# Transposing q and k on VectorE in 32x32 squares instead of on TensorE, in a fused attention and SwiGLU kernel

## The chip, the core and the metric

The kernel runs on one NeuronCore of a Trainium2 chip. The metric is the device time of one execution in microseconds (us), here the median of three runs.

The engines have short names in the profile: PE is TensorE (PEld its weight loads), DVE is VectorE, ACT is ScalarE, POOL is GpSimd, SP is SyncE, which computes nothing and issues most of the DMA transfers. The transfers themselves are carried out by 16 DMA engines.

## The reference

Attention with a threshold, 8 batches of 8 heads, 576 positions of 64, all float32; then a SwiGLU layer over the 4,608 rows of 512 that the heads make together.

```python
scores = scale * np.matmul(q, k.transpose(0, 1, 3, 2))          # 576 x 576 per head
thresh = np.max(scores, axis=-1, keepdims=True) - tau           # tau = 0.02
scores = np.where(scores >= thresh, scores, -1000000000.0)
attn = np.exp(scores - np.max(scores, axis=-1, keepdims=True))
attn = attn / (np.sum(attn, axis=-1, keepdims=True) + 1e-09)
x = np.matmul(attn, v)                                          # -> (B * S, H * D)
xn = x / rms(x) * rms_g
out = (silu(xn @ w_gate) * (xn @ w_val)) @ w_out                # 512 -> 1536 -> 512
```

## The kernel before, in words

**Tiling.** Heads are worked on in pairs, p = 0 to 3 (one head on partitions 0 to 63, the other on 64 to 127). Of the 576 rows of a batch 512 are "main" and 64 are the "tail". The main rows make four chunks of 128 queries; the tails of two batches together make one more chunk. So there are 36 chunks, and 36 x 4 pairs = 144 steps, in the order of `chunks` and `steps` (L249 to L263). A step is one chunk of queries of one head pair against all 576 keys.

**A step.** TensorE makes the scores of both heads (L601). From step 32 to step 143 this is done in bursts of 1,024 columns per head that fill `s_ps`, two times two PSUM banks; the next burst can start when VectorE has read the last one. VectorE copies the scores out and takes their minimum after a scale of -1/8 (L634). POOL adds tau (L675). ScalarE, and POOL for one head in every third step, make the weights (L686, L693, L705, L719, L724) in `wsb`, of which there are three. SP issues a DMA transpose of the weights into `wt`, of which there are five (L753; the first 16 steps use TensorE). TensorE multiplies them by v (L771, L776), VectorE normalises (L793, L794).

**The layer behind it.** When a chunk's four steps are done, ScalarE, POOL and a DMA transpose (L823) make its normalised, transposed rows. Groups of four chunks (two at first) then go through the layer: TensorE L877 and L882, ScalarE L891, VectorE L894 and L899, TensorE L948 (L923 in the last, streamed group), an eviction at L961 or L963, and a store at L968, or L972 for a tail chunk.

**How q and k get there.** TensorE needs both with the 64 elements of a head on the partitions. For batches 1 to 7 `emit_qk` (L307) loads k and q of a pair by one transfer each, 128 partitions by 8 pieces of 64 float32 (L316), into one of three buffers `qkn`. TensorE transposes them by 16 matmuls with an identity, 64x64 each (L326), into two banks of a ring of PSUM banks. VectorE copies one bank into `qkt` (L339), ScalarE the other (L337). The k tails of a batch are loaded by one transfer and transposed by `emit_k_tail` (L456, L461, L473), the q tails of two batches by `emit_q_tail` (L481, L485, L495). Batch 0 has its own code, `emit_first` (L347).

**How v gets there.** `emit_v` (L501) loads v of a pair by one transfer of 128 partitions by 2 pieces of 1 KB (L521), and the tails by two transfers (L533); POOL casts to float16 (L509).

**What sets the order.** Every operation is an `Op` with an engine, an assumed cost (`COST`, `DMA_NS`), a due step (`prio`) and the operations it depends on. `order_ops` (L55) plays a list schedule with these costs and writes down one fixed order per engine; `RANK` (L26) shifts the due steps of kinds of operations, for those due from step 8 on. Each engine then runs its order strictly, waiting at an instruction until its operands are there. SP's order holds the loads, the transposes of L753 and L823, and the stores. A load of a batch's inputs is held back to a step (`gated`, and L1057): `emit_batch_inputs` (L544) sets 3.3 steps from pair to pair, and loads three steps ahead of that. The buffers of `qkn` are free for a new load when the transposition three blocks back is done. TensorE's score matmuls run either over 128 queries at once or over two times 64 (`o.quad`, L1065); the first is taken where another operation with half-height tiles, such as a transposition, follows.

Of the kernel before, what the change touches and what calls it, by code (L numbers as in the profile page):

```python
# [19 lines left out]
    pool_tiny=302.0, pool_mean=944.0, pool_dma=880.0, cast_v=620.0, cast_vt=475.0, cast_w=665.0,  # L20
    sp=420.0, sp_v=600.0, sp_w=600.0, sp_tr=1300.0, sp_qk=680.0, sp_tl=630.0,
)
DMA_NS = dict(qk=1250.0, tl=700.0, v=880.0, vt=350.0, wt=1700.0, xt=800.0, out=800.0, w=820.0, wo=2500.0)
SWITCH = 125.0

RANK = dict(  # L26
    ACT={"emit_ffn/ev": -70, "emit_ffn/store": 10, "emit_ffn/tanh": -150, "emit_k_tail/ev": 60, "emit_q_tail/ev": -60, "emit_qk/ev": -20,
        "emit_softmax/ex": 70, "emit_softmax/ex2": 63, "emit_softmax/prelu": 140, "emit_x/sq": -20},
    DVE={"emit_av/half": -110, "emit_burst/ttr": 14, "emit_ffn/ev": -100, "emit_ffn/silu": 20, "emit_k_tail/ev": -70, "emit_qk/ev": 16,
        "emit_softmax/ev": 50},  # L30
    PE={"emit_burst/fn": -29, "emit_ffn/gmm": 8, "emit_ffn/omm": 10, "emit_ffn/vmm": -34, "emit_k_tail/tr": -100, "emit_q_tail/tr": 100, "emit_qk/tr":
        -10, "emit_softmax/tr": -130},
    POOL={"emit_softmax/mask": 60, "emit_softmax/nthr": 60, "emit_softmax/take": -10, "emit_x/mean": 110, "emit_x/norm": -60, "round_/<lambda>": 90,
        "main/<lambda>": 150, "main/cast": 10},
)
# [19 lines left out]
def order_ops(ops, ring_sizes):  # L55
# [4 lines left out]
    for o in ops:  # L60
        if o.prio >= 8.0 and o.eng != "SP":
            path = o.fn.__qualname__.split(".")
            o.prio += RANK[o.eng].get((path[-3] if path[-3].startswith(("emit", "load", "setup", "transposed", "round")) else "main") + "/" + path[-1], 0.0)

# [15 lines left out]
    out = []  # L80
    ready_at = {i: 0.0 for i in range(len(ops))}
    while len(out) < len(ops):
# [35 lines left out]
        if o.ring is not None:  # L118
            o.slot = []
            for _ in range(o.nring):  # L120
                got = min(f for f in ring_free[o.ring] if f[1] in (o.pick or SLOTS))
                ring_free[o.ring].remove(got)
                o.slot.append(got[1])
        eng_free[e] = t + cost
        if o.dma:
# [21 lines left out]
def kernel(  # L147
# [29 lines left out]
    def ps(name, n):  # L177
# [9 lines left out]
    wo = sb("wo", [128, NFC, DM], FP16)  # L187
    qkn = [sb(f"qkn{i}", [128, 2, 4, 2, D]) for i in range(NQK)]
    qtl = [sb(f"qtl{i}", [128, H, D]) for i in range(2)]
    ktl = [sb(f"ktl{i}", [128, H, D]) for i in range(2)]  # L190

    qkt = [sb(f"qkt{i}", [128, NP, 2 * S]) for i in range(2)]
    qkT = [[t[:, p].rearrange("p (j s) -> p j s", j=2)[:, :, 0:MAIN].rearrange("p j (c n) -> p j c n", n=128)
            for p in range(NP)] for t in qkt]
    kT = [[[t[:, p, S:2 * S], t[:, p, MAIN:MAIN + S]] for p in range(NP)] for t in qkt]
    kTt = [[t[:, :, S + MAIN:2 * S], t[:, :, MAIN:S]] for t in qkt]
    qTv = [sb(f"qTv{i}", [128, NP, 128]) for i in range(2)]
    va = [sb(f"va{i}", [128, NP, 10, D + 1], FP16) for i in range(2)]
# [107 lines left out]

    def emit_qk(b, p, prio):  # L307
        dst = qkT[b % 2][p]
        n = len(tr_of[0])
# [11 lines left out]
        def tr(o):  # L321
            for j in (1, 0):
                for c in range(4):
                    for r, rs in enumerate(HALF):
                        at = 256 * j + 64 * c
                        nc.tensor.transpose(ring[o.slot[r]][:, at:at + 64],  # L326
                                            nat[rs, j, c].rearrange("s h d -> s (h d)"), id32[rs, rs])
# [16 lines left out]
        for c in range(4):  # L344
            qk_ready[b, p, c] = done

    def emit_first():  # L347
# [63 lines left out]
        def emit_k(p, load, prio):  # L411
            nat = qkn[p % NQK]
            t, k_ready[p] = transposed(load, [pair(nat[:, 1, c]) for c in range(4)],
                                       [(0, 2, qkT[0][p][:, 1, 0:2]), (2, 2, qkT[0][p][:, 1, 2:4])], prio,
                                       [("ACT" if p in (1, 2) else "DVE", 0, 2), ("ACT", 2, 4)])
            tr_of[1].append(t)

        emit_k(0, lo, -20)
        _, q0_ready[0] = transposed(lq, [pair(q0[:, 0:2])], [(0, 1, qkT[0][0][:, 0, 0:1])], -21, [("DVE", 0, 1)])
        tk, kt_first = transposed(lt, [pair(ktl[0][0:64, 0:2])], [(0, 1, kTt[0][h][HALF[h], 0:1]) for h in range(2)], -19, [("ACT", 0, 1)])  # L420
# [3 lines left out]
        tq, got = transposed(lq2, [pair(q0[:, 2 * p:2 * p + 2]) for p in range(1, NP)],  # L424
                             [(p - 1, 1, qkT[0][p][:, 0, 0:1]) for p in range(1, NP)], -9, [("DVE", 0, 1), ("ACT", 1, 3)])
        q0_ready[1:] = [got[:1], got[1:], got[1:]]
# [8 lines left out]
        for p in range(NP):  # L435
            nat = qkn[p % NQK]
            t, got = transposed(load_q(p, (-23, -22, -19, -18)[p]), [pair(nat[:, 0, c]) for c in range(1, 4)],
                                [(0, 3, qkT[0][p][:, 0, 1:4])], p + 2.0, [(EVAC[p % 2], 0, 3)])
            tr_of[0].append(t)
            for c in range(4):  # L440
                qk_ready[0, p, c] = k_ready[p] + (got if c else q0_ready[p])
# [59 lines left out]
    def emit_v(b, prio):  # L501
# [13 lines left out]
        for p in range(NP):  # L515
# [4 lines left out]
            def load(o, p=p, nat=nat):  # L520
                nc.sync.dma_start(out=nat, in_=main[:, 2 * p:2 * p + 2])  # L521

            lo = gated(add("SP", COST["sp_v"], pr, v_cast[n - len(vst):n - len(vst) + 1] if n >= len(vst) else [], load,
                           dma=DMA_NS['v'], bulk=True), pr)
# [5 lines left out]
            if p == 0:  # L530
                def load_tail(o):
                    for e in range(2):
                        nc.sync.dma_start(out=vtl[64 * e:64 * e + 64], in_=hv[e, MAIN:S])  # L533

                lo = gated(add("SP", 2 * COST["sp_tl"], pr + 0.3, vt_cast[-2:], load_tail, dma=DMA_NS['vt'], bulk=True), pr + 0.3)
                for e in range(2):
                    es = slice(64 * e, 64 * e + 64)
                    ca = add("POOL", COST["cast_vt"], (pr + 1.3 if b else -0.5), [lo] + [x for p in range(NP) for x in free(p)],
                             round_(t[es, :, 8 + e, 0:D], vtl[es]))
                    vt_cast.append(ca)  # L540
                    for p_ in range(NP):
                        v_ready.setdefault((b, p_), []).append(ca)

    def emit_batch_inputs(b):  # L544
        base = first_step[b - 1] if b else -10
        if b == 1:
            base += B1_BASE
        emit_tail_load(b, base + (4 if b else 1))
        if b == 0:
            q0_use.extend(emit_first())  # L550
        else:
            for p in range(NP):
                pr = base + 3.3 * p + 3
                emit_qk(b, p, pr)
                if p == 0:
                    emit_k_tail(b, pr + 2)
        emit_v(b, base + 5 if b else -1)
        if b % 2:
            emit_q_tail(b // 2, v_step[b // 2] - 1.5)
# [9 lines left out]
    def parts_of(s):  # L569
        ci, p = steps[s]  # L570
        kind, b, c = chunks[ci]
        if kind == "m":
            deps = qk_ready[b, p, c] + kt_ready[b, p]
            whole = [(slice(0, 128), b % 2, lambda hs: qkT[b % 2][p][hs, 0, c])]
            quads = [(rs, b % 2, lambda hs, rs=rs: qkT[b % 2][p][hs, 0, c, rs]) for rs in HALF]
            return deps, whole, quads
        deps = list(qv_ready[b])
        quads = []
        for e in range(2):
            deps += qk_ready[2 * b + e, p, 0] + kt_ready[2 * b + e, p]  # L580
            quads.append((HALF[e], e, lambda hs, e=e: qTv[b % 2][hs, p, HALF[e]]))
        return deps, None, quads
# [4 lines left out]
    def emit_burst(segs, prio, runs):  # L587
# [5 lines left out]
        for run in runs:  # L593
            def fn(o, run=run):
                for s, lo, hi, at in run:
                    _, whole, quads = info[s]
                    p = steps[s][1]
                    for rows, i, lhs in quads if no_whole or o.quad else whole:
                        for h in range(2):
                            hs = HALF[h]  # L600
                            nc.tensor.matmul(s_ps[h][rows, at:at + hi - lo], lhs(hs), kT[i][p][h][hs, lo:hi],  # L601
                                             start=True, stop=True)
# [251 lines left out]
    def emit_ffn(slot, parts, ready_step, pace, streamed):  # L854
# [81 lines left out]
        for j, (ci, _) in enumerate(parts):  # L936
# [28 lines left out]
            def store(o, oi=oi, kind=kind, b=b, c=c, late=late):  # L965
                if kind == "m":
                    dst = out[b * S:b * S + MAIN].rearrange("(si sc) d -> si sc d", sc=4)[:, c]
                    (nc.scalar if late else nc.sync).dma_start(out=dst, in_=osb[oi])  # L968
                else:
                    for e in range(2):  # L970
                        r0 = (2 * b + e) * S + MAIN
                        nc.sync.dma_start(out=out[r0:r0 + TAIL], in_=osb[oi][64 * e:64 * e + 64])  # L972

# [141 lines left out]
NSTAGE = 3  # L1115
NQK = 3
W_FROM = 2.0
W_STEP = 0.4
# [42 lines left out]
```

## Time and profile before

| what | value |
|---|---|
| three runs | 547.73, 549.47, 551.49 us; median 549.47 |
| the profiled execution: its own time | 549.99 us |
| its span (first to last instruction) | 548.0 us |
| granted TensorE clock | 0.998 of full speed |
| POOL busy | 256.4 us (47%) |
| DMA packets | 270,022, of which 252,544 under 512 B |
| read from and written to HBM | 37.75 and 9.44 MB |
| block loads (L316), issue to landing | 3.4 / 4.3 / 7.8 us (shortest, median, longest) |
| weight transposes (L753), issue to landing | 3.2 / 3.6 / 7.8 us |
| who waited for the weight transposes | POOL 1.1 us, ACT 0.7 us |
| longest waits by kind | POOL L675 for VectorE 169.9 us; VectorE L634 for TensorE L601 39.1 us; ScalarE L891 for TensorE L877 31.2 us |

How to read the profile. "Busy" is the time in which an engine's instructions ran, whatever they waited for inside. Matmuls are pipelined, so that a busy TensorE isn't TensorE at its peak. A group's line gives source line, engine, operation, output and inputs with shape, count, then busy us and mean ns of one, then idle time of the engine just ahead of such instructions. A DMA queue's line gives packets, megabytes, and the time that its packets took as a share of all 16 engines over the span or window; q1 holds what SP issues, q10 what ScalarE issues. The sum of packets in flight can pass 1.0. The chain of work is followed back from the last instruction, at each step to what released it.

### The profile page before, as it was taken

To read this page: it belongs to the slowest core of one execution; us is meant where nothing else is said; L and a number is where in the kernel's file an instruction comes from. 1 tells how busy PE (TensorE), PEld (TensorE's weight loads), DVE (VectorE), ACT (ScalarE), POOL (GpSimd) and SP (SyncE) were. 2 spreads that over 40 slices of the span, in tenths; PEclk is the share of its full clock that TensorE was granted. 3 is DMA by queue.
4 is the path that set the end of the run, shared out by engine and by line. 5 is a ranking of instruction groups with operands and counts; after the bars stand their busy time and mean duration, and the time that the engine had idled before them with its cause. 6 is when DMAs were issued, how large, how long until landed. Compare 5 with 4: busy or idle time off the path is not lost.

```text
span 548.0 us, 14515 instructions
## 1 busy us (share of the span) xinstructions
PE 536.8 (98%) x5420; PEld 295.8 (54%) x5420; DVE 452.7 (83%) x1300; ACT 441.8 (81%) x684; POOL 256.4 (47%) x418
## 2 busy tenths in 40 slices
PE   8998999999999999999999999999999999999996
PEld 4765676664555455645555556555655454545442
DVE  4997998888997799789987998699979987995562
ACT  5998989988998789788979898879988988793221
POOL 2367833763645434654554454644644544451000
PEclk9999999999999999999999999999999999999999
DMA  8999999979997797998898789999998567564201
GB/s 195 262 256 277 185 177 224 144 164 200 181 161 160 153 155 160 202 194 148 173 196 165 111 160 206 220 171 166 175 202 151 104 97 150 92 127 82 79 0 77
DMA packets 270022, 89.03 MB, mean 162 GB/s; under 512 B 252544, under 2 KB 262272, under 8 KB 269952
## 3 DMA queue, kind: packets, MB, share of 16 engines
q1 hardware_dynamic: 267024, 85.76, 81.9%
q0 software_dynamic: 1600, 1.57, 2.0%
q8 instruction: 42, 0.69, 0.5%
q10 hardware_dynamic: 1328, 0.79, 0.5%
q14 instruction: 28, 0.23, 0.2%
HBM read 37.75 MB, written 9.44 MB: 86 GB/s over the span
## 4 chain that ended last, share of the span: by engine, by line
PE 80%; DVE 5%; DMA 4%; POOL 4%; issue 3%; ACT 3%; SPq 0%; POOLq 0%; DVEq 0%; ACTq 0%
PE s_ps L601 25%; PE ring L948 14%; PE ring L877 14%; PE ring L882 14%; PE ring L776 5%; DVE ssb L634 3%; PE ring L771 2%; PE ring L326 2%; PE s_ps L923 2%; DMA stg<-in_moe_w_gate_dram 1%; POOL wsb L719 1%; ACT ssb L686 1%; DMA vst<-in_v_dram 1%; PE s_ps L882 1%; POOL wsb L724 1%
## 5 line engine op out<-in xcount | busy, mean ns | idle before, releaser
L686 ACT ACTIVATE ssb<-ssb,nth 128x576 f32<-128x576 f32 x246 | 180.8, 766 | 28.1 <-POOL nth L675 27.5
L634 DVE CUSTOM_DVE_ANT_0 ssb<-s_ps,zrow 128x576 f32<-128x576 f32 (+8 forms) x288 | 172.0, 635 | 10.6 <-PE s_ps L601 8.8
L601 PE MATMUL s_ps<-qkt 64*64 64x288 f32 (+17 forms) x1636 | 154.7, 415 | 1.8 <-DVE mx L634 1.1
L693 ACT ACTIVATE wsb<-ssb 128x1152 f16<-128x1152 f32 x102 | 118.2, 1159 | 1.6
L675 POOL TENSOR_SCALAR nth<-mx 128x2 f32<-128x2 f32 x144 | 31.6, 219 | 178.0 <-DVE mx L634 169.9
L877 PE MATMUL ring<-xnT,wg 128*128 128x512 f16 (+1 forms) x472 | 111.1, 358 | 0.1
L601 PEld LDWEIGHTS s_ps<-qkt 64*64 64x64 f32 (+1 forms) x1636 | 77.8, 146 | 60.2 <-issue 26.0
L882 PE MATMUL ring<-xnT,wv 128*128 128x512 f16 (+1 forms) x456 | 107.0, 357 | 0.5 <-DVE qkt L339 0.3
L891 ACT ACTIVATE th<-ring 128x512 f32<-128x512 f32 (+1 forms) x118 | 63.9, 541 | 31.6 <-PE ring L877 31.2
L894 DVE SCALAR_TENSOR_TENSOR sl<-th,ring 128x512 f32<-128x512 f32 (+1 forms) x118 | 73.9, 628 | 13.8 <-ACT th L891 13.5
L634 DVE CUSTOM_DVE_ANT_0 ssb<-s_ps,zrow,mxp 128x128 f32<-128x128 f32 (+7 forms) x112 | 53.4, 514 | 31.0 <-PE s_ps L601 30.3
L719 POOL TENSOR_SCALAR wsb<-ssb,nth 128x576 f16<-128x576 f32 x42 | 72.5, 1726 | 4.8 <-DMA wt<-wsb 1.1
L882 PEld LDWEIGHTS <-wv 128*128 128x128 f16 x480 | 45.6, 98 | 49.8 <-issue 6.4
L877 PEld LDWEIGHTS <-wg 128*128 128x128 f16 x480 | 42.8, 97 | 40.7 <-issue 4.4
L724 POOL TENSOR_TENSOR wsb<-wsb,esb 128x576 f16<-128x576 f16 x42 | 53.7, 1278 | 6.1 <-ACT esb L705 3.1
L776 PE MATMUL ring<-va,wt 128*128 128x65 f16 (+1 forms) x1264 | 50.3, 193 | 0.0
L776 PEld LDWEIGHTS <-wt 128*128 128x128 f16 (+1 forms) x1280 | 46.2, 100 | 3.0 <-issue 0.4
L948 PE MATMUL ring<-wo,hf 128*128 128x512 f16 x204 | 47.5, 379 | 0.0
L899 DVE TENSOR_TENSOR hf<-ring,sl 128x512 f16<-128x512 f32 (+1 forms) x59 | 37.3, 635 | 4.5 <-PE s_ps L601 0.5
L948 PE MATMUL ring<-wo,stg 128*128 128x512 f16 x168 | 39.1, 379 | 0.0
L705 ACT ACTIVATE esb<-ssb,nth 128x576 f16<-128x576 f32 x42 | 32.3, 770 | 7.9 <-POOL nth L675 7.9
L899 DVE TENSOR_TENSOR stg<-ring,sl 128x512 f16<-128x512 f32 (+1 forms) x55 | 34.6, 631 | 4.0
(76 smaller groups left out, 552.8 us busy)
## 6 DMA issues: line engine op xcount, KB each, us to landing
vst<-in_v_dram SPq DMA_DIRECT2D x32, 256.0 KB, 3.4
qkn<-in_k_dram SPq DMA_DIRECT2D x31, 256.0 KB, 4.3
out_dram<-osb SPq DMA_DIRECT2D x29, 256.0 KB, 2.9
qkn<-in_q_dram SPq DMA_DIRECT2D x28, 256.0 KB, 4.5
stg<-in_moe_w_gate_dram SPq DMA_DIRECT2D x6, 512.0 KB, 6.3
stg<-in_moe_w_val_dram SPq DMA_DIRECT2D x6, 512.0 KB, 5.9
wt<-wsb SPq DMA_TRANSPOSE x128, 3.6
wo<-in_moe_w_out_dram POOLq DMA_DIRECT2D x4, 384.0 KB, 6.3
```

The lines of the kernel that those rows point to most:

```text
L601: nc.tensor.matmul(s_ps[h][rows, at:at + hi - lo], lhs(hs), kT[i][p][h][hs, lo:hi], start=True, stop=True)
L634: nc.vector.tensor_tensor_reduce(out=ssb_of(s)[:, h, lo:hi], in0=s_ps[h][:, at:at + hi - lo], in1=zrow[:, lo:hi], scale=-1.0 / 8.0, scalar ...
L686: nc.scalar.activation(out=sb_[:, h], in_=sb_[:, h], func=PRELU, scale=-1.0, bias=nth[m][:, h:h + 1], **PRELU_KW)
L693: nc.scalar.activation(out=wsb[s % NW], in_=sb_, func=AF.Exp)
L719: nc.gpsimd.tensor_scalar(out=wsb[s % NW][:, h], in0=sb_[:, h], scalar1=nth[m][:, h:h + 1], scalar2=None, op0=ALU.is_le)
L776: nc.tensor.matmul(ring[o.slot[0]][rs, at:at + D + 1], w[:, 5 * h + j, rs], va[vi][:, p, 2 * j + h], start=False, stop=(h == 1 and j == 3))
L877: nc.tensor.matmul(ring[o.slot[0]][:, 0:n], wg[d][:, fs], xnT[slot][:, d, 0:n], start=(d == 0), stop=(d == 3))
L882: nc.tensor.matmul(ring[o.slot[0]][:, 0:n], wv[d][:, fs], xnT[slot][:, d, 0:n], start=(d == 0), stop=(d == 3))
L891: nc.scalar.activation(out=th[i][:, 0:n], in_=ring[g.slot[0]][:, 0:n], func=AF.Tanh, scale=0.5)
L894: nc.vector.scalar_tensor_tensor(out=sl[i][:, 0:n], in0=th[i][:, 0:n], scalar=1.0, in1=ring[g.slot[0]][:, 0:n], op0=ALU.add, op1=ALU.mult)
L899: nc.vector.tensor_tensor(out=hf[hi][:, 0:n], in0=ring[vv.slot[0]][:, 0:n], in1=sl[i][:, 0:n], op=ALU.mult)
L948: nc.tensor.matmul(ring[(first or o).slot[0]], hf[hs[fc][0]][:, 128 * j:128 * (j + 1)], wo[:, fc], start=(fc == 0), stop=(fc == NFC - 1))
```

## The change

From batch 2 on (`BLOCKED = 2`) `emit_qk` hands over to `emit_blocks`. Each head's q and k are loaded by a transfer of its own, 64 partitions by 18 pieces of 32 float32: partition 32 e + s takes half e (32 elements) of the 18 rows 18 s to 18 s + 17. The main part and the tail come together. Three VectorE transposes of 32x32 squares then write `qkt`: one for k, one for q (512 columns each), one for the tails of both (192 columns). The buffers `qkn` become `qkx`, 1,216 float32 wide; `qkt` gets 64 more columns, and k now stands ahead of q in it.

The queries and keys of a chunk are therefore other rows than before, and v and the output follow: v of a pair is loaded by two transfers, each of 4 times 32 pieces of 1 KB in DRAM, its tails by four transfers of 32 partitions, and a chunk is stored as 4 times 32 rows (a tail chunk as 2 times 32 for each of its batches). The separate loads and TensorE transposes of the tails are gone for batches 2 to 7, and TensorE reads the queries of tail chunks from `qkt`.

Two more edits: where an operation takes several PSUM banks from a given list (the last group's four accumulators), it takes them in rising order ("banks sorted"); and `COST`, `DMA_NS` and the whole of `RANK` have other values, so that the written-down order differs on every engine. The diff, cut to its core:

```diff
+    qkx = [sb(f"qkx{i}", [128, 2 * S + TAIL]) for i in range(NQK)]
+    qkt = [sb(f"qkt{i}", [128, NP, 2 * S + TAIL]) for i in range(2)]
+    RUN = S // 32
+    LEAD = (0, RUN - MAIN // 32)
+    TAIL_AT = (MAIN // 32, 0)
+    def rows_of(x):
+        return x.rearrange("(s r) d -> s r d", r=RUN)
...
     def emit_qk(b, p, prio):
+        if b >= BLOCKED:
+            return emit_blocks(b, p, prio)
...
+    def tails(x):
+        return bass.AP(tensor=x.tensor, offset=x.offset, ap=[list(x.ap[0]), [S, 3], [1, TAIL]])
+    def emit_blocks(b, p, prio):
+        n = len(tr_of[0])
+        nat = qkx[n % NQK]
+        before = [x for j in range(2) for x in tr_of[j][n - NQK:n - NQK + 1]] if n >= NQK else []
+        free = last_s.get(("k", b - 2, p), [])
+        los = {}
+        for j, src in ((1, k), (0, q)):
+            for h in range(2):
+                at = S + TAIL if j == 0 else 0 if h else TAIL
+                def load(o, src=src, h=h, at=at):
+                    nc.sync.dma_start(out=nat[HALF[h], at:at + S].rearrange("p (r d) -> p r d", d=32),
+                                      in_=rows_of(src[b, 2 * p + h]).rearrange("s r (e d) -> e s r d", d=32))
+                los.setdefault(j, []).append(gated(add(
+                    "SP", COST["sp_qb"], prio - 3, before, load, dma=DMA_NS["qkb"], bulk=True), prio - 3))
+        def emit_turn(j):
+            def turn(o):
+                at = TAIL if j else S + TAIL
+                nc.vector.transpose(out=qkt[b % 2][:, p, at:at + MAIN].rearrange("p (c k d) -> p c k d", c=4, d=32),
+                                    in_=nat[:, at:at + MAIN].rearrange("p (k c d) -> p c k d", c=4, d=32))
+            return gated(add("DVE", COST["turn"], prio, los[j] + free, turn), prio)
+        def turn_tails(o):
+            nc.vector.transpose(out=tails(qkt[b % 2][:, p]), in_=tails(nat))
...
-                nc.sync.dma_start(out=nat, in_=main[:, 2 * p:2 * p + 2])
+                if b < BLOCKED:
+                    nc.sync.dma_start(out=nat, in_=main[:, 2 * p:2 * p + 2])
+                    return
+                for h in range(2):
+                    nc.sync.dma_start(out=nat[:, h], in_=rows_of(v[b, 2 * p + h])[:, LEAD[h]:LEAD[h] + MAIN // 32].rearrange(
+                        "s (k c) d -> k s c d", c=4))
...
+                        if b >= BLOCKED:
+                            for t in range(2):
+                                at = 64 * e + 32 * t
+                                nc.sync.dma_start(out=vtl[at:at + 32], in_=v[b].rearrange(
+                                    "(a e) (s r) d -> e r s a d", e=2, r=RUN)[e, TAIL_AT[e] + t])
+                            continue
...
-                if p == 0:
+                if p == 0 and b < BLOCKED:
                     emit_k_tail(b, pr + 2)
...
+                        dst = rows_of(out[b * S:b * S + S])[:, 0:MAIN // 32].rearrange("s (k c) d -> c k s d", c=4)[c]
...
+                        if 2 * b >= BLOCKED:
+                            dst = rows_of(out[r0:r0 + S])[:, MAIN // 32:RUN].rearrange("s t d -> t s d")
...
+            if o.pick:
+                o.slot.sort()
+BLOCKED = 2
```

## The prediction, made before the changed kernel ran

> **What bounds the kernel now.** I read the page first: its head, the busy times, the queue that carries nearly all transfers, and the chain of work that ended last.
>
> ```profile
> span 548.0 us, 14515 instructions
> ...
> PE 536.8 (98%) x5420; PEld 295.8 (54%) x5420; DVE 452.7 (83%) x1300; ACT 441.8 (81%) x684; POOL 256.4 (47%) x418
> ...
> q1 hardware_dynamic: 267024, 85.76, 81.9%
> ...
> PE 80%; DVE 5%; DMA 4%; POOL 4%; issue 3%; ACT 3%; SPq 0%; POOLq 0%; DVEq 0%; ACTq 0%
> ```
>
> TensorE is busy 98% of the span and is 80% of the chain: it is the bound. But q1, SP's queue, keeps the 16 DMA engines busy 81.9% of the time as well. The change touches the stretch from about 82 to 413 us, where batches 2 to 7 are loaded and transposed (the tenths of L326 show its first four blocks before 60 us, the next from 82 us, the last at 409 us). So I asked for windows; the columns are stretch, length, busy us of PE, PEld, DVE, ACT and POOL, granted clock, DMA share, GB/s.
>
> ```profile
> 82.00:413.00 331.00, 329.94 (x3427) 181.29 (x3426) 287.28 (x855) 289.31 (x446) 170.96 (x267) 1.00 0.95 175
> 367.00:394.00 27.00, 27.00 (x260) 14.72 (x252) 26.08 (x78) 25.48 (x41) 14.93 (x25) 1.00 1.02 173
> ```
>
> PE works 329.94 of 331 us at full clock, VectorE 287.3, and the DMA engines are at 0.95. In the 27 us of the second row VectorE holds 96.6% while PE loses nothing. What the change takes away and what is nearest to what it adds stand in the groups of that stretch:
>
> ```profile
> L326 PE MATMUL ring<-id,qkn 64*128 64x64 f32 x368 | 16.0, 223 | 0.0
> ...
> L461 PE MATMUL ring<-id,ktl 64*128 64x64 f32 x24 | 2.5, 223 | 0.0
> L485 PE MATMUL ring<-id,qtl 64*128 64x64 f32 x16 | 0.8, 222 | 0.0
> ```
>
> ```profile
> L339 DVE COPY qkt<-ring 128x512 f32<-128x512 f32 x24 | 16.4, 685 | 0.0
> ...
> L634 DVE CUSTOM_DVE_ANT_0 ssb<-s_ps,zrow 128x192 f32<-128x192 f32 x12 | 3.8, 352 | 0.0
> ...
> L473 DVE COPY qkt<-ring 64x256 f32<-64x256 f32 x6 | 2.6, 427 | 0.2
> ```
>
> Last, the DMA view of two short windows, for the price of a packet. From 0 to 10 us ScalarE's queue holds one load alone; from 500 to 510 us there are three stores and one transpose.
>
> ```profile
> q10 hardware_dynamic: 1040, 0.26, 11.5%
> ```
>
> ```profile
> DMA packets 976, 0.92 MB, mean 92 GB/s; under 512 B 592, under 2 KB 592, under 8 KB 976
> ...
> q1 hardware_dynamic: 976, 0.92, 27.0%
> ```
>
> The first load is 128 rows of 8 pieces of 256 B: 1,024 packets, and 1,040 are counted. The 16 more are one end mark for each of 16 engines: the transfer was dealt to all 16, 8 whole rows to each. A packet of 256 B costs 0.115 x 16 x 10 us / 1,040 = 17.7 ns of an engine. In the second window 43.2 us of engine time less 592 x 17.7 ns leaves 85.2 ns for each of 384 packets of 2,048 B. A straight line through the two gives 46.6 ns for 1,024 B and 12.9 ns for 128 B.
>
> **The change part by part.** The sums are made against the profiled execution, 549.99 us: 548.0 of span and 2.0 around it. It is 0.5 above the median of the three runs, 549.47.
>
> TensorE loses L326, L461 and L485 in the stretch: 16.0 + 2.5 + 0.8 = 19.3 us, all on the path. ScalarE loses its half of the evictions (13.5 us at L337, 2.2 at L473, 1.3 at L495), off the path.
>
> VectorE loses 16.4 (L339) and 2.6 us (L473) and gains, 24 times, two turns of 128x512 and one of 128x192. No row shows a turn. Bounds: 0.43 us (L473, half the columns) and 0.75 (a 128x576 reduction at L634). I take 0.685, the copy of as many float32 elements, and 0.352 for the tails: 24 x (2 x 0.685 + 0.352) = 41.3, net +22.3. VectorE then needs 309.6 us where PE needs 329.9 - 19.3 = 310.6. At the 96.6% that it has held, that is 320.5 us for the stretch instead of 331. A turn waits for its load; behind it in VectorE's order stand the score reductions (L634), and TensorE's next score burst waits for those, since one pair of banks serves all bursts.
>
> SP issues, for the 24 blocks, 96 loads for 60 (48 at L316, 12 tails), V loads in two (24 more), V tails in twice as many (12 more): 36 x 0.65 + 24 x 0.58 + 12 x 0.62 = +45 us of issue in 331. They stand in SP's one order with the transposes of the weights (L753). Nobody on PE waits for L753 now, so this hides behind the lead that those have, and costs some of it.
>
> The transfers themselves decide. A block's q and k were 2 x 1,024 packets of 256 B and its share of the tails 256 more; now they are 4 x 1,152 packets of 128 B. In 24 blocks 55,296 packets become 110,592. Dealt evenly, an engine had 3,456 x 17.7 ns = 61 us and gets 6,912 x 12.9 = 89: +28 us, 0.09 of share on top of 0.95.
>
> But are they dealt evenly? The new pattern in DRAM is "e s r d": its outermost step counts 2. The V loads count 4 there, the stores 4, the tail stores 2. Every transfer of the trace counts 64 rows or more, and where its marks can be counted each of 16 engines got whole outermost rows. No row shows a smaller count. The bounds are 16 engines, as in all rows, and as many as there are outermost rows: 2 for q and k. I take 2, because shares of whole rows are what the nearest row (1,040 packets) shows; 16 is kept for the other end. Then two engines carry 55,296 packets each:
>
> - q and k: 55,296 x 12.9 ns = 713 us (489 if a packet goes by its bytes, 8.85 ns; 979 if by number, 17.7 ns).
> - what those engines carry already in the stretch, 0.95 x 331 = 314, less the 61: 253.
> - V, 6,144 packets of 1 KB on 4 engines, so 1,536 each for 384: 1,152 x 46.6 ns = 54.
> - stores on 4 and 2 engines: 24 chunks of 128 rows, 768 each for 192, and 3 tail chunks, 192 for 24: 576 and 168 packets x 85.2 ns = 63, two thirds of it in the stretch: 42.
>
> Sum 1,062 us where the stretch had 331. PE's 311 and VectorE's 310 hide under it. What was hidden stops hiding: a weight transpose issued behind a block's loads waits 4 x 576 x 12.9 ns = 30 us on those two engines, wsb and wt have 3 and 5 buffers, so scores, ScalarE and TensorE stop within a few steps. 549.99 - 331 + 1,062 = **1,281 us**.
>
> [...]
>
> **The rivals.**
>
> *All 16 engines share.* For it: every transfer counted here. Then DMA share rises by 0.09 and VectorE sets the stretch: 549.99 - 331 + 320.5 = 540 us. At best PE is the limit (311: 530 us); at worst VectorE keeps the 86.8% that it has now (309.6 / 0.868 = 357: 576 us). It ends faster by over 1% if VectorE holds over 95% (309.6 us in a stretch under 325.5). Against it: no transfer here has so few outer rows.
>
> *Two engines, but others each time.* Evenly loaded in sum, each load lands after 576 x 12.9 ns = 7.4 us plus the 3.2 that 4.3 us of landing leave beyond 64 packets of 17.7 ns: 10.6 us. Loads go out 3 steps ahead, near 10 us, and a block's four come together. If VectorE waits 2 us at each of 24 blocks: 540 + 48 = 588. Nothing in the rows speaks for it or against it.
>
> *Two engines, and idle ones too.* Loads wait for buffers and steps, and steps for transposes. If the two engines stand idle one landing (4 us) per block: 1,281 + 96 = 1,377. Against it: three buffers of q and k.
>
> **How the numbers follow.** Two fixed engines 0.84 (the last rival within it), changing pairs 0.04, 16 engines 0.12; of these 12 in 100, 7 end faster by over 1%, 3 within 1%, 2 slower. The 1% is about what a measurement of this kernel can tell from no change. Faster 0.07, same 0.03, slower 0.90. The range is that of the two-engine case: low 489 + 253 + 54 + 42 = 838, less 87 if the rest costs 17.7 ns a packet and not the 26.9 of the whole run's q1 row (81.9% of 16 x 548 us over 267,024): 751, so 970 us, taken as 960; high 979 + 253 + 96 = 1,328, so 1,547, and 1,600 with half a landing idle per block. That leaves out some 2 in 10, nearly all of it below.
>
> **What would show it.** Right: the stretch of blocks is some three times as long, PE under 40% busy in it; the queue's share falls well under 0.5 though two engines never rest; the block loads land after 15 us or more, not 4.3; waits on DMA for qkx on VectorE and for wt on TensorE; before 82 us and after the last load little changes. Turns near 0.69 us, 48 of 512 columns and 24 of 192. Wrong: landings near 4 to 5 us and a span near 540 with VectorE over 94% busy. The price of a 128 B packet could be off by a third either way without touching the case.

## The result, and the profile after

The changed kernel takes 1,057.04 us in the median of four runs (1,055.33 to 1,060.62) beside 549.55 for the kernel before: a ratio of 1.924, 95% interval 1.916 to 1.933. The forecast was 1,281, between 960 and 1,600. The profiled execution took 1,060.62 us.

The page of the changed kernel, its lines on the span, the engines, SP's queue and the chain of work that ended last:

```profile
span 1058.8 us, 14380 instructions
...
PE 628.5 (59%) x5336; PEld 312.4 (30%) x5336; DVE 472.5 (45%) x1342; ACT 428.7 (40%) x648; POOL 257.3 (24%) x418
...
q1 hardware_dynamic: 321204, 85.75, 47.5%
...
SPq 33%; DMA 30%; PE 16%; issue 7%; ACT 6%; DVE 4%; POOL 3%; POOLq 0%; DVEq 0%; ACTq 0%
```

No computing engine bounds it any more. TensorE fell from 98% to 59% and from 80% of the chain to 16%; SP's queue of instructions and the transfers hold 63% of the chain. The 16 DMA engines together are less busy than before (47.5% against 81.9%), so "the transfers" cannot mean all of them. The windows, with the same columns as before (stretch, length, busy of PE, PEld, DVE, ACT, POOL, granted clock, DMA share, GB/s):

```profile
0.00:82.00 82.00, 69.07 (x805) 45.87 (x805) 60.15 (x174) 60.76 (x97) 40.67 (x82) 0.96 0.87 196
82.00:413.00 331.00, 181.78 (x1523) 90.34 (x1523) 135.54 (x394) 126.79 (x193) 74.18 (x116) 0.73 0.45 76
413.00:900.00 487.00, 248.79 (x1956) 114.96 (x1957) 180.36 (x524) 161.95 (x237) 100.14 (x154) 0.73 0.45 70
```

In the 331 us that held 3,427 matmuls before there are now 1,523. Nearly all the lost time lies where blocks are loaded: 487 of the 511 us that the span grew; the other 24 come after 900 us. What the engines wait for, over the whole run, from the view of waits (total us, times, longest):

```profile
PEld L839 <- DMA wt<-wsb: 311.3, 58, 21.9
...
POOL va L564 <- DMA vst<-in_v_dram: 260.5, 23, 26.5
...
DVE qkt L385 <- DMA qkx<-in_q_dram: 123.9, 14, 12.7
```

The weight transposes, for which no engine waited more than 1.1 us in total before, are now TensorE's main wait; v and q come late too. SP itself is held at its instructions. Those that issue a block's loads (duration shortest, median, longest in ns) took 634 (k) and 701 ns (q) in the median before, 2,475 at most:

```profile
L376 SPq DMA_DIRECT2D qkx<-in_k_dram x48: 513/580/12070, 50.3 to 877.6; - x48
L376 SPq DMA_DIRECT2D qkx<-in_q_dram x48: 512/5369/7629, 62.9 to 885.3; - x48
```

The plainest view is the DMA view of 20 us in the middle (300 to 320 us). Each figure of the second line is the rate of half a microsecond:

```profile
DMA  1111111111111111111111111111111792222699
GB/s 27 28 27 27 27 27 24 19 27 27 27 27 26 26 27 26 27 27 27 27 27 27 27 27 27 27 27 27 27 35 20 165 196 61 82 92 92 141 287 251
```

For 15 us the 16 engines are busy for between one and two tenths of their time, at a flat 27 GB/s; as soon as the block loads are through, the rate goes up to 287. If 27 GB/s is two engines, one moves 13.5 GB/s, a packet of 128 B each 9.5 ns. That the number is two is shown next.

### The profile page after: what moved, and what is told of

The parts are those of the page before. It is cut to its first block, busy times and chain, and to the rows that moved or that the text cites. A ratio compares the mean times of both kernels' runs of the same rounds, so it can differ in the third digit from the quotient of the medians.

```text
span 1058.8 us, 14380 instructions
## 1 busy us (share of the span) xinstructions
PE 628.5 (59%) x5336; PEld 312.4 (30%) x5336; DVE 472.5 (45%) x1342; ACT 428.7 (40%) x648; POOL 257.3 (24%) x418
## 3 DMA queue, kind: packets, MB, share of 16 engines
q1 hardware_dynamic: 321204, 85.75, 47.5%
## 4 chain that ended last, share of the span: by engine, by line
SPq 33%; DMA 30%; PE 16%; issue 7%; ACT 6%; DVE 4%; POOL 3%; POOLq 0%; DVEq 0%; ACTq 0%
DMA wt<-wsb 18%; SPq L376 16%; SPq L821 11%; PE s_ps L669 5%; SPq L580 4%; DMA vst<-in_v_dram 4%; DMA out_dram<-osb 4%; PE ring L945 3%; PE ring L1016 3%; ACT ssb L754 3%; DMA qkx<-in_k_dram 2%; PE ring L950 2%; DVE ssb L702 2%; SPq L891 1%; PE ring L844 1%
## 5 line engine op out<-in xcount | busy, mean ns | idle before, releaser
L839 PE MATMUL ring<-va,wt 128*128 128x130 f16 (+1 forms) x160 | 35.9, 251 | 321.0 <-DMA wt<-wsb 272.3
L669 PE MATMUL s_ps<-qkt 64*64 64x288 f32 (+9 forms) x2176 | 194.4, 468 | 45.9 <-DVE mxp L702 23.9
L945 PE MATMUL ring<-xnT,wg 128*128 128x512 f16 (+1 forms) x464 | 128.7, 406 | 24.9 <-DMA xnT<-xn 21.1
L385 DVE STREAM_TRANSPOSE qkt<-qkx 128x512 f32<-128x512 f32 x48 | 33.9, 707 | 222.3 <-DMA qkx<-in_q_dram 123.9
L669 PEld LDWEIGHTS s_ps<-qkt 64*64 64x64 f32 (+1 forms) x2176 | 91.7, 154 | 129.2 <-issue 42.8
L950 PE MATMUL ring<-xnT,wv 128*128 128x512 f16 (+1 forms) x460 | 128.2, 408 | 1.3 <-DVE sl L962 1.3
L839 PEld LDWEIGHTS <-wt 128*128 128x128 f16 (+1 forms) x160 | 14.9, 104 | 333.8 <-DMA wt<-wsb 311.3
L758 ACT ACTIVATE wsb<-ssb 128x576 f16<-128x576 f32 x42 | 28.5, 680 | 145.7 <-DMA wt<-wsb 145.4
L564 POOL TENSOR_SCALAR va<-vst 128x512 f16<-128x512 f32 x32 | 20.1, 628 | 260.9 <-DMA vst<-in_v_dram 260.5
L844 PE MATMUL ring<-va,wt 128*128 128x65 f16 (+1 forms) x1280 | 67.5, 213 | 0.0
L844 PEld LDWEIGHTS <-wt 128*128 128x128 f16 (+1 forms) x1280 | 59.1, 114 | 22.5 <-issue 20.4
```

What stands on the lines that cost most here:

```text
L669: nc.tensor.matmul(s_ps[h][rows, at:at + hi - lo], lhs(hs), k_of(bb, p, h)[hs, lo:hi], start=True, stop=True)
L844: nc.tensor.matmul(ring[o.slot[0]][rs, at:at + D + 1], w[:, 5 * h + j, rs], va[vi][:, p, 2 * j + h], start=False, stop=(h == 1 and j == 3))
L945: nc.tensor.matmul(ring[o.slot[0]][:, 0:n], wg[d][:, fs], xnT[slot][:, d, 0:n], start=(d == 0), stop=(d == 3))
L950: nc.tensor.matmul(ring[o.slot[0]][:, 0:n], wv[d][:, fs], xnT[slot][:, d, 0:n], start=(d == 0), stop=(d == 3))
```

## The experiments

Each kernel is timed beside the kernel before (549.1 to 549.9 us in these sets).

**1. q and k dealt to all engines (e_qk16).** Each load becomes two, so that the outermost step in DRAM counts 576 rows and not 2.

```diff
-                    nc.sync.dma_start(out=nat[HALF[h], at:at + S].rearrange("p (r d) -> p r d", d=32),
-                                      in_=rows_of(src[b, 2 * p + h]).rearrange("s r (e d) -> e s r d", d=32))
+                    for e in range(2):
+                        rs = slice(64 * h + 32 * e, 64 * h + 32 * e + 32)
+                        nc.sync.dma_start(out=nat[rs, at:at + S].rearrange("p (r d) -> p r d", d=32),
+                                          in_=rows_of(src[b, 2 * p + h])[:, :, 32 * e:32 * e + 32])
```

> Each q or k load of 64 partitions becomes two of 32 partitions, whose outermost step in DRAM counts 576 and no longer 2; the bytes and the 110,592 packets of 128 B stay, and so do the loads of v and the stores. Theory (the time went into two engines that carry all of q and k): an engine then carries 6,912 of these packets and not 55,296; at the 9.4 ns each that the changed kernel's trace shows where two are in flight, 65 us and not 520. v (54 us) and the stores (42 us) stay on four and two engines, on top of the other 253: 414 us of engine time in a stretch that had 331, if nothing of it overlaps, so 549 to 640 us, and 590 as one number. First rival (small packets as such, or the number of packets, cost the time): it stays above 950. Second rival (SP's order becomes the bound, since it issues 96 loads more at 0.55 us, 53 us on top of the 45 already added): over 620, with SP never waiting for anything in the stretch.

Measured: 669.05 us (ratio to before 1.217, 1.214 to 1.219). The same bytes in the same packets of 128 B cost 388 us less, so neither their size nor their number had cost that time by itself. SP's queue on the page:

```profile
q1 hardware_dynamic: 324084, 85.76, 79.1%
```

There are 324,084 - 321,204 = 2,880 packets more, and the data are the same. The prediction had read the 16 packets beyond the data of one load as end marks, one on each engine that carried it. In the packed trace they are packets of 4 B: 7,604 on this queue in the changed kernel and 10,484 here, while the packets of every other size agree in number. 192 loads on 16 engines make 3,072 marks, 96 loads on two make 192: the difference is 2,880 exactly. The q and k loads of the changed kernel were dealt to two engines. The packets in flight say the same: of those of 128 B never more than four are open at once in the changed kernel, and up to 32 here, two for each engine. The 669 lies 29 us above the theory's upper end; the second rival's sign is there as well, since SP's instructions fill 414 of the 448 us from 82 to 530.

**2. Only v and the stores dealt evenly (e_vst16).** The turn writes the 32 columns of a square four apart, so that v and the stores of a chunk have 32 outermost rows. Tail stores become two transfers each.

```diff
-                nc.vector.transpose(out=qkt[b % 2][:, p, at:at + MAIN].rearrange("p (c k d) -> p c k d", c=4, d=32),
+                nc.vector.transpose(out=qkt[b % 2][:, p, at:at + MAIN].rearrange("p (c d k) -> p c k d", c=4, d=32),
...
-                        "s (k c) d -> k s c d", c=4))
+                        "s (k c) d -> s k c d", c=4))
```

> Only v and the stores are dealt evenly (the turn writes columns 4 apart, outermost step 32), while q and k stay on the outermost step of 2. Theory: q and k keep 520 us of two engines' time and v and the stores give back at most 54 + 42 us less 12 that come back evenly spread: 84 us at most, so 970 to 1,050, and 990 as one number. Rival (the stores and v are what blocks the order, since weight transposes stand behind them): below 900.

Measured: 976.96 us (1.776, 1.772 to 1.781): 80 us less than the changed kernel, where at most 84 were expected. The marks agree here too:

```profile
q1 hardware_dynamic: 322224, 85.76, 44.8%
```

That is 1,020 more: 48 v loads x (16 - 4), 22 chunk stores on SP x (16 - 4), and 12 tail stores on 16 for 6 on two, so 576 + 264 + 180 = 1,020.

**3. Everything dealt evenly (e_all16).** Both edits together.

> As the kernel with the split q and k loads, and also the turn writes the 32 columns of a square 4 apart, so that v of a head and a chunk's store have 32 outermost rows and not 4; tail stores are split in two. Now every transfer but none has an outermost step of 16 or more. Theory: this is the rival of the prediction in which all 16 engines share, 540 us (530 to 576), plus what the additional 96 issues on SP cost: 535 to 600. It tells whether transposing on VectorE pays once the transfers are even: faster than before by over 1% only if VectorE holds over 95% in the stretch. Rival (something other than the dealing of transfers costs the time: the new order, the waits on VectorE): over 650.

Measured: 596.36 us (1.086, 1.081 to 1.091). Of the 507 us that the change cost, 461 were the dealing; the two edits alone had given 388 and 80. The 461 are what is left after two costs that this kernel adds: 96 more loads to issue on SP, and slower turns (1,124 ns, not 707). But 47 us are left over the kernel before, and the first rival's 540 isn't reached. Experiments 5 to 12 look for those 47. The chain of this kernel, called the even kernel from here on:

```profile
PE 35%; DMA 19%; SPq 11%; ACT 11%; DVE 10%; issue 9%; POOL 5%; DVEq 0%; POOLq 0%; ACTq 0%
```

**4. Two engines still, but larger packets (e_big2).** The loads keep their outermost step of 2 and their bytes.

```diff
-                    nc.sync.dma_start(out=nat[HALF[h], at:at + S].rearrange("p (r d) -> p r d", d=32),
-                                      in_=rows_of(src[b, 2 * p + h]).rearrange("s r (e d) -> e s r d", d=32))
+                    nc.sync.dma_start(out=nat[HALF[h], at:at + S],
+                                      in_=rows_of(src[b, 2 * p + h]).rearrange("s (e r) d -> e s (r d)", e=2))
```

> The q and k loads keep their outermost step of 2 and their bytes, but fetch 64 runs of 2,304 B instead of 1,152 pieces of 128 B; the elements that land in the squares are others, so the outputs differ from the reference. Theory (two engines, and a price per packet): 3,072 packets on each of two engines at 66 to 95 ns (84 ns for 2,048 B in the trace, by its bytes, and 0.7 of that where two are in flight) are 200 to 290 us where 55,296 packets of 128 B were 520. The time falls by 230 to 320 us, to 740 to 830. Rival (two engines, and a price per byte): 1,057 stays. Rival (the count of two does not matter, small packets do): 540 to 576.

Measured: 812.52 us (1.477, 1.473 to 1.482), as the theory of two engines with a price per packet had it. The DMA view of the same 20 us (300 to 320) shows plateaus of ones again, at nearly twice the rate:

```profile
DMA  4333932996019911111111117999139911111111
GB/s 129 108 100 85 188 74 54 216 206 114 14 28 215 113 46 51 51 46 55 46 55 46 55 34 170 281 293 180 5 69 209 54 46 51 46 55 46 55 46 55
```

Half of some 50.5 GB/s is 25 GB/s, 91 ns for 2,304 B. The time says the same: 55,296 x 9.5 = 525 us less the 244.5 saved leaves 281 us for 3,072 packets, 91 ns each.

**5. The net VectorE work alone, added to the kernel before (e_dve).**

```diff
                     nc.vector.tensor_copy(out=dst[:, :, :, rs], in_=src)
+                    if b >= 2:
+                        nc.vector.transpose(out=nat[:, 1].rearrange("p c h d -> p (c h d)"), in_=nat[:, 0].rearrange("p c h d -> p (c h d)"))
+                        nc.vector.transpose(out=nat[:, 1].rearrange("p c h d -> p (c h d)")[:, 0:192],
+                                            in_=nat[:, 0].rearrange("p c h d -> p (c h d)")[:, 192:384])
```

> The kernel before, in its own order, plus the net VectorE work of the change and nothing else of it: behind VectorE's eviction of each block of batches 2 to 7 one turn of 128x512 and one of 128x192, of data that TensorE has already read, into a place that nobody reads; 24 x (0.707 + 0.354) = 25.5 us. TensorE keeps its transpositions. The prediction's step (VectorE can hold 96.6%, so work of this size hides under TensorE): 312 of 331 us in the stretch, 548 to 553. Rival (VectorE keeps the 86.8% of before): the stretch needs 360 us, so 565 to 580.

Measured: 558.14 us (1.018, 1.014 to 1.023): 8 us for 26 us of work. It lies between the two: VectorE neither hides it all nor falls back to its old share.

```profile
82.00:413.00 331.00, 327.45 (x3355) 183.63 (x3354) 301.24 (x880) 282.72 (x434) 168.06 (x263) 1.00 0.92 170
```

In the same 331 us VectorE is now busy 301.24 (91%), and TensorE got 72 matmuls less far (3,355 against 3,427).

**6. SP's extra issues alone, added to the kernel before (e_sp).**

```diff
+                if b >= 2:
+                    for i in range(2):
+                        nc.sync.dma_start(out=tiny[4 * (p % 2) + 2 * j + i], in_=src[b, 2 * p, 0:16, 0:16])
```

> The kernel before, in its own order on every engine, plus two loads of 16 pieces of 64 B behind each q and each k load of batches 2 to 7 (96 in all, 6 KB per block, into tiles that nobody reads). Theory (what is left of the loss once all transfers are even is SP's issuing: 347 of 378 us in the even kernel's stretch against 272 of 331 before): 96 x 0.58 = 56 us more make 328 of 331; at the 92% that SP reached in the even kernel the stretch needs 356 us, so 575 us, 562 to 590. Rival (SP's issuing is hidden and the loss comes from VectorE or from the transfers): 547 to 555.

Measured: 562.5 us (1.026, 1.022 to 1.029): 13 us for 96 issues (the bytes that come with them are 0.1 of 85.9 MB), at the very lower edge of the theory and well above the rival. The wait for weight transposes, 1.8 us in all before, is back: POOL's alone is

```profile
POOL wsb L723 <- DMA wt<-wsb: 9.0, 12, 2.0
```

**7. A corrected cost for planning the order (e_plan).** The even kernel was planned with 0.6 us for a pair of loads that take twice 0.63.

```diff
-                    "SP", COST["sp_qb"], prio - 3, before, load, dma=DMA_NS["qkb"], bulk=True), prio - 3))
+                    "SP", 2 * COST["sp_qb"], prio - 3, before, load, dma=DMA_NS["qkb"], bulk=True), prio - 3))
```

> The kernel with even transfers, all loads on SP, but the written-down order is planned with the 1.2 us that a pair of split loads takes to issue, and not 0.6. Theory (too many issues, not their order): 585 to 605. Rival (the order was wrong because the assumed cost was): 555 to 575.

Measured: 595.83 us (1.086, 1.082 to 1.090). This assumed cost wasn't it. The rest of the order is not ruled out: `COST` and `DMA_NS` kept their old entries in the change and gained four, but `RANK` is new as a whole, and no run here has the kernel before with the new `RANK` or the changed one with the old.

**8. Three quarters of the turns left out of the even kernel (e_turn128).**

```diff
-                nc.vector.transpose(out=qkt[b % 2][:, p, at:at + MAIN].rearrange("p (c d k) -> p c k d", c=4, d=32),
-                                    in_=nat[:, at:at + MAIN].rearrange("p (k c d) -> p c k d", c=4, d=32))
+                nc.vector.transpose(out=qkt[b % 2][:, p, at:at + 128].rearrange("p (d k) -> p k d", d=32),
+                                    in_=nat[:, at:at + MAIN].rearrange("p (k c d) -> p c k d", c=4, d=32)[:, 0])
```

> The kernel with even transfers, its q and k turns cut from 512 columns to 128; three quarters of the transposition are left out, so the outputs differ from the reference. VectorE loses 48 x (1.12 - 0.28) = 40 us; SP, the transfers and TensorE keep their work. Theory (SP's order binds alone): 588 to 600. Rival (VectorE's turns are what the rest of the loss is): 555 to 575. Both bind in turn: 575 to 588.

Measured: 596.37 us (1.088, 1.082 to 1.093), with 34 us less of turns on VectorE (19.7 against 53.9). No change: as long as SP issues all loads, VectorE isn't what ends last. SP's instructions fill 347 of 378 us (82 to 460) with the turns and without them; before they filled 272 of 331.

**9. k loads issued by ScalarE (e_act16).** The even kernel, with `nc.scalar` for k and `nc.sync` for q.

> The kernel with even transfers, its 96 k loads issued by ScalarE and not by SP; the order is planned with 1.2 us for a pair of loads and not 0.6. SP falls by 58 us to some 290 of the stretch, ScalarE rises from 272 by about as much, to 330. Theory (SP's order is what the even kernel waits for): faster than it, 555 to 580, with ScalarE now the fullest engine after TensorE. Rival (VectorE's 330 us, with turns of 1.12 us where the first had 0.71, set the time): 590 to 600, no change.

Measured: 611.83 us (1.117, 1.112 to 1.123): slower than with all loads on SP and outside both ranges, so the expectation failed. SP did drop out, from 11% of the chain in the even kernel (8% in e_plan, which is planned with the same 1.2 us) to 1%:

```profile
PE 44%; DVE 19%; ACT 13%; DMA 13%; issue 5%; POOL 2%; SPq 1%; ACTq 1%; DVEq 0%; POOLq 0%
```

ScalarE pays 0.58 us per issue, 54 us in the stretch, ahead of work that others need at once. Two of its waits, 11.2 us together, were for a transfer of k. That its order, and not its load, makes the kernel slower is only argued.

**10. k loads issued by POOL (e_pool16).** The same with `nc.gpsimd` for k.

> The kernel with even transfers, its 96 k loads issued by POOL's queue, which has 170 of 378 us busy, and not by SP. At 0.86 us each, as POOL's four loads of w_out took, 83 us. Theory (SP's issuing is worth about what 56 us of it cost the kernel before, 13 us): 575 to 590. Rival (POOL's in-order wait for a buffer holds up the weights behind it, as ScalarE's did): over 600.

Measured: 573.84 us (1.045, 1.042 to 1.047): 22.5 us less than the even kernel and 22.0 less than e_plan, a little under the theory's 575. SP has 96 issues, some 60 us, less. But it isn't certain that the whole gain is SP's, because the transfers changed too: in POOL's queue k goes in larger packets, 1,536 of 4,096 B and 1,536 of 512 B where there were 55,296 of 128 B. POOL's queue in the even kernel, and here:

```profile
q0 software_dynamic: 1600, 1.57, 1.9%
```

```profile
q0 software_dynamic: 6208, 8.66, 9.0%
```

In e_act16 k's packets had stayed at 128 B. No run relieves SP without one or the other: larger packets, or k's issues in ScalarE's order. The chain has changed hands:

```profile
PE 42%; DVE 26%; DMA 13%; POOL 6%; issue 6%; ACT 5%; SPq 1%; DVEq 0%; POOLq 0%; ACTq 0%
```

VectorE went from 10% (17% in e_plan) to 26%. The turn that writes four apart costs it 1,133 ns in this kernel where the contiguous one took 707.

**11. Another choice of rows, contiguous turns (e_rows).** Partition s takes rows s, s + 32, and so on, so a chunk is 128 consecutive rows; v, its tails and the stores are even of themselves, and k is still issued by POOL.

```diff
-        return x.rearrange("(s r) d -> s r d", r=RUN)
+        return x.rearrange("(r s) d -> s r d", r=RUN)
...
-                                    in_=nat[:, at:at + MAIN].rearrange("p (k c d) -> p c k d", c=4, d=32))
+                                    in_=nat[:, at:at + MAIN].rearrange("p (c k d) -> p c k d", c=4, d=32))
...
+                    r0 = 32 * LEAD[h]
+                    nc.sync.dma_start(out=nat[:, h].rearrange("s (c d) -> s c d", d=D),
+                                      in_=v[b, 2 * p + h, r0:r0 + MAIN].rearrange("(c s) d -> s c d", c=4))
...
+                        dst = out[b * S + 128 * c:b * S + 128 * c + 128]
```

> As the kernel with even transfers and k loads issued by POOL, but partition s takes rows s, s + 32, s + 64, ... of its head and not 18 rows in a run. A chunk then holds 128 consecutive rows, so v (512 pieces of 256 B per head, not 128 of 1 KB), v's tails (two transfers per batch, not four) and the stores have 64 outermost rows or more without any stride in what the turn writes. The turn is the contiguous one of the changed kernel: 0.71 us and not 1.13, 20 us less for VectorE; SP issues 12 transfers less. Theory (with SP relieved, VectorE is next: 26% of the chain of waits, and 25.5 us of such work cost the kernel before 8): 555 to 568. Rival (what is left is SP's or POOL's issuing): 570 to 575. Faster than the kernel before: under 545, which would need VectorE at 94% of the stretch.

Measured: 556.20 us (1.012, 1.010 to 1.015), 17.6 below the last, where VectorE lost 20 us of work. That VectorE's time counts nearly in full once SP is relieved fits, but the figure also holds 12 transfers less on SP, smaller pieces of v and another written-down order. It is the best form of the transposition on VectorE found here, 1.9 times as fast as the change as made, and still 1.2% slower than the kernel before. Of the 47 us, some 22 went with k's loads and 18 with this step; the last 6 stay unexplained.

```profile
82.00:420.00 338.00, 323.11 (x3326) 163.88 (x3324) 297.21 (x886) 271.86 (x406) 227.91 (x351) 0.99 1.11 168
```

TensorE is at 96% of the stretch, VectorE at 88%. The DMA share is 1.11, so a share of 0.95 was no sign of full engines: it sums packets that overlap.

**12. Banks sorted, alone (e_sort).** The kernel before with `o.slot.sort()` for the listed banks.

> The kernel before with the one edit that an operation which takes several banks from a given list takes them in rising order. All theories: it concerns four accumulators of the last group, 547 to 552 us, no difference that can be measured.

Measured: 547.46 us (0.997, 0.995 to 0.999). That is 0.3% less, at most half a per cent by the interval, and below the 1% that counts here; no version beat the kernel before by more.

## Why the prediction was right, and where its working was off

**The dealing: right.** The step was "as many as there are outermost rows: 2 for q and k", 4 for v and the stores, 2 for tail stores. The marks show this, by 2,880 and 1,020 exactly. They count engines: that an engine gets whole rows (8 of 128 in the first load, with its 16 marks) is an inference from them, and which row went where no trace here shows. The 16 of all the rows before was no evidence for a row count of 2, since none had one. That all loads of q and k share one pair, as the sum of 1,281 takes it, no run had shown before. The rival of changing pairs (588) missed by 469 us. And the trace of the changed kernel shows loads in turn: SP issued one of k and two of q from 296.59 to 308.36 us, and their marks come in twos, at 303.4 and 303.8, 309.2 and 309.3, 314.6 and 314.8 us. Each load's last mark comes 5.4 to 5.5 us behind that of the load before, and the rate stays at the 27 GB/s of one pair. Which two engines they are no trace here shows.

**The price of a packet: mis-sized.** The forecast lay 220 us above the profiled execution (1,281 against 1,060.62), and this step made 188 of them: "q and k: 55,296 x 12.9 ns = 713 us". The packets' records are that long (13.3 ns in the mean), but up to four of them are open at once, two per engine, so that an engine is through one every 9.5 ns: 525 us. With that the sum is 1,281 - 188 = 1,093. The step's lower bound of 8.85 ns would have met the measured 1,057 to the microsecond; that is luck, since it goes by bytes, and by bytes the 2,304 B of experiment 4 would cost 159 ns and not 91. The price came from a queue's share, which adds up records that overlap. The same holds for "0.95 x 331 = 314" of load already carried; by how much wasn't measured. v and the stores were close: 54 + 42 = 96 us in the sum, at most 84 by the expectation of experiment 2, and 80 measured.

**What stops hiding: right, but for SP.** The weight transposes are the longest wait of the changed kernel (311.3 us, 21.9 at most, where 30 were forecast for one). Two things were not foreseen. POOL's casts wait 260.5 us for v. And SP does not only have its transposes land late: its own instructions take longer (those that issue q 5,369 ns in the median and not 701), so that SP is 33% of the chain. What holds them is open.

**TensorE's 19.3 us: only part arrives.** In the best form TensorE's busy time falls by 6.9, from 536.8 to 529.9 us. The working overlooked that score matmuls run over 128 queries only where a half-height operation follows (L1065). With the transpositions gone 64 of them do so and not 412; there are 2,240 instead of 1,892, and they take 177.8 us instead of 173.1. The other 8 us stay open in part: the groups' rows overlap (those of TensorE before add up to 631 us, where it was busy for 536.8), so a group's row is no measure of what its removal sets free.

**"At the 96.6% that it has held", and "this hides": both wrong.** On the kernel before, 26 us of VectorE work alone cost 8 us, and 56 us of issuing on SP alone cost 13. VectorE had held 96.6% over 27 us, not over 331. So the first rival's 540 was out of reach even with even transfers: 596 as the loads stand, 556 at best. Dealt evenly, the change would still have been slower, by far less, in every form tried.

**What would show it.** Right: the stretch 2.5 times as long (82 to 900 us; "some three times"), the waits for wt and for qkx (222.3 us), turns of 707 and 354 ns where 685 and 352 were taken. Half right: the queue's share fell, but to 0.45 in the stretch and not well under 0.5. Wrong: TensorE is busy 55% and 51% in it, not under 40%, since the stretch is shorter and each matmul longer; and the first 82 us do change (805 matmuls, not 902), with the first blocks' loads out at 50 us. The landing times can't be told: the trace of this run lists none for any transfer on SP's queue.

## What to carry to other kernels

Before a transfer's pattern is rewritten, count its outermost step in DRAM: with 2 there, each block load ran on two of 16 engines, and the kernel (v and the stores on four) took 1.92 times as long; the same bytes of q and k in the same packets, dealt to 16, took 388 us less. The share of a queue cannot show it: in the same 20 us (300 to 320) it was 40.2% in the changed kernel and 97.3% in experiment 4, both with the loads of q and k on two engines; the rate in short windows (27 GB/s, flat) and the count of packets (end marks) can. And work that is moved off a bound engine is not hidden when the engines that take it, here VectorE at 87% and SP's issuing at 82% of the stretch, are nearly as full: each alone cost a quarter to a third of what was added.

## What the hardware showed that was not expected

**Price against size.** Two engines carried packets of 128 B at 13.5 GB/s each and packets of 2,304 B at 25: 9.5 ns against 91.

**In these runs the granted clock was lower where TensorE was busy less.** From the pages (TensorE's busy share, mean granted clock): 98%, 0.998 before; 96%, 0.992 in e_rows; 90%, 0.989 in the even kernel and 0.969 in e_act16; 84%, 0.939 in e_qk16; 72%, 0.871 in e_big2; 63%, 0.796 in e_vst16; 59%, 0.776 in the changed kernel. Which of the two brings the other down no run here separates. The gate matmuls took 358 ns in the mean before (first line), and 406 in the changed kernel:

```profile
L877 PE MATMUL ring<-xnT,wg 128*128 128x512 f16 (+1 forms) x472 | 111.1, 358 | 0.1
```

```profile
L945 PE MATMUL ring<-xnT,wg 128*128 128x512 f16 (+1 forms) x464 | 128.7, 406 | 24.9 <-DMA xnT<-xn 21.1
```

TensorE's busy time grew by 92 us, though its transpositions are gone. As it is 16% of the chain, little of the 507 us is likely to come from this; how much wasn't measured.

**A turn that writes four apart** took 1,124 ns in the even kernel; the contiguous one, on the same 128x512, 700:

```profile
L387 DVE STREAM_TRANSPOSE qkt<-qkx 128x512 f32<-128x512 f32 x48 | 53.5, 1124 | 14.4 <-DMA qkx<-in_k_dram 6.9
```

```profile
L387 DVE STREAM_TRANSPOSE qkt<-qkx 128x512 f32<-128x512 f32 x48 | 33.2, 700 | 8.4 <-DMA qkx<-in_q_dram 5.7
```

The first line is of the even kernel, the second of e_rows.
